# Stepping w_out's conversions at every slice behind the attention, with the PSUM banks split three and two

## The chip, the cores and the metric

The kernel runs on one core of one Trainium2 chip. The metric is the device time in microseconds of one execution; a lower time is better. The core has five engines with queues of their own, each of which runs its instructions strictly in the order in which the program gives them: TensorE (matmuls; its results go to PSUM, which has eight banks), VectorE, ScalarE, GpSimd, and SyncE, which starts most transfers. An engine whose next instruction waits for another engine stands still, whatever is queued behind.

## The reference, cut to what matters

Three layers in a row, on 2 batches of 768 tokens:

```python
# 1: retention ("attention"), 8 heads of 64
state = gamma * state + k[t] (outer) v[t];  y[t] = scale * q[t] @ state
# 2: gated feed-forward on x = y, d_model 512, d_ff 1024
h = relu(x @ w_in)
conv = sum(conv_w[k] * h[tokens shifted by k - 1] for k in range(3))
x2 = (h * sigmoid(conv)) @ w_out
# 3: top-1 mixture of 8 experts on x2, with a sticky choice:
#    a token takes argmax(x2 @ w_gate), or the expert of the token before it
#    where sigmoid(x2 @ w_local) >= 0.5
out = p[e] * (relu(x2 @ w1[e]) @ w2[e])
```

## The kernel before

Products run on values cut into a high and a low part (`hi`, `lo`), three matmuls for each product (`mm3`, lines 126 to 128). The order of all work is written out by hand: generators are stepped, and each step issues a few instructions.

**The pieces around the change.**
- `first = stream(0, range(8))` is the w_in product of batch 0: 8 blocks m of 128 hidden columns, each two halves `u` of 384 tokens, each of four slices (`ffn_in`, L347). A slice is one `mm3` of the 128x384 form; the fourth of a half is followed by ScalarE's relu (L357). A half takes one tile `h_ps` of the pool `psa`.
- Behind each slice `tick` steps `hidden(b, m)` (L327) for the blocks whose w_in product is done, at the slices TIMES = 0, 1, 3, 4, 10, 11, 13, 15 after it: ScalarE's first tap into `cc` (L331), two more taps on VectorE (L334), the sigmoid on ScalarE (L336), the product with h on VectorE (L338), the cut into `hg` high (ScalarE L307) and low (VectorE L311), and the router's logit on TensorE (`logit`, L325: eight matmuls). `cc` has two buffers. `logit` keeps a list `owed`: a block whose gate weights aren't in `ready` stays there until `logit` is called again.
- `convert` (L152) is one conversion of a 128x512 block of w_in or w_out from its 64-bit words: a load (three buffers `raw`), two VectorE instructions (L142, L143), one on ScalarE (L144), an addition on GpSimd (L146), the high part on ScalarE (L164), the low part on GpSimd (L166). Those of w_out (m = 0 to 7) go on: four transposes on TensorE into `wt_ps` (L175), ScalarE's copy to `wt` (L179), the product with the gate's weights into `wc_ps` (L183, eight matmuls), ScalarE's copy to `wc` (L185). The list `turning` lets one block at a time through this part. `wt_ps` and `wc_ps` have the same tag "g" in the pool `psg`. The numbers that a `convert` yields say after how many calls of `advance` it goes on.
- `advance` (L384) steps all conversions in `running` by one.

The attention's loop has 50 turns, each with one `advance`; from its turn 25 on, slices of `first` are put between (20 by its end). Then the attention's PSUM pools are closed and new ones opened: `psa` with 4 banks for `h_ps`, `psg` with 1, `psb` with 2 for w_out's product; one more bank holds the logits. The other 44 slices of `first` follow, with one `advance` behind every second one, then `while running: advance()` until no conversion is left.

After that come `stream(1, range(1))` (block 0 of batch 1, eight slices), `flush(0)` (the remaining `hidden` steps of batch 0), the w_out product of batch 0 (`ffn_out`, L454: first two token tiles over the blocks 0 to 5, then the rest) with `route(0)` between, `stream(1, range(1, 8))`, the same for batch 1 with `route(1)` and `tables()`, and the experts. `route` (L482) takes four tiles `sp` for the sticky choice from `psa` and `et` from `psg`; `tables` takes three from `psg`.

Of the kernel before, what the change touches and what calls it, by code (L numbers as in the profile page):

```python
# [9 lines left out]
F32 = mybir.dt.float32  # L10
# [6 lines left out]
PSUM = bass.MemoryType.PSUM  # L17
# [6 lines left out]
P = 128  # L24
# [60 lines left out]
def tile_kernel(ctx, tc, cat, cst, qT, kT, kN, vN, w_in, conv_w, w_out, wg, w1, w2, out):  # L85
# [4 lines left out]
    def pool(name, bufs, stack=ctx, **kw):  # L90
        return stack.enter_context(tc.tile_pool(name=name, bufs=bufs, reuse_waits="tile", **kw))

    def stack():
        return ctx.enter_context(ExitStack())
# [14 lines left out]
    psg = pool("psg", 1, ps_stack, space=PSUM)  # L109
    psa = pool("psa", 1, ps_stack, space=PSUM)  # L110
# [204 lines left out]
    def logit(*block):  # L315

        owed.extend(block)
        while owed and owed[0][1] in ready:
            b, m = owed.pop(0)
            if m == 0:  # L320
                LG[b] = psl.tile([P, NG, 32], F32, name="lg")
            x = CC.pop((b, m)).rearrange("p (t n) -> p t n", n=P)
            for i in range(4):
                o = slice(32 * i, 32 * i + 32)
                te.matmul(LG[b][o], wc[:, m, :], x[:, :, o], start=(m == 0), stop=(m == 7), skip_group_check=True)  # L325
# [58 lines left out]
    def advance():  # L384
        for r in list(running):
            r[1] -= 1
            if r[1] <= 0:
                r[1] = next(r[0], 0)
                if not r[1]:
                    running.remove(r)  # L390
# [42 lines left out]
        slices += 1  # L433
    ps_stack.close()
    q_stack = stack()
    psa = pool("psa", 4, q_stack, space=PSUM)
    psg = pool("psg", 1, q_stack, space=PSUM)
    psb = pool("psb", 2, q_stack, space=PSUM)
    n = 0
    for _ in first:  # L440
        n += 1
        if n % 2 == 0:
            advance()
    while running:
        advance()
    p1_stack.close()
# [35 lines left out]
    def route(b):  # L482

        logit(*[(b, m) for m in range(8) if (b, m) in CC and (b, m) not in owed])
        l = rt.tile([P, NG, 32], F32, name="l")
        ve.transpose(out=l.rearrange("p t e -> p (t e)"), in_=LG.pop(b).rearrange("p t e -> p (t e)"))
        wide = lambda a: a.unsqueeze(2).to_broadcast([P, NG, E])
        mx = rt.tile([P, NG], F32, name="mx")
        ve.tensor_reduce(out=mx, in_=l[:, :, 0:E], axis=AX.X, op=ALU.max)
        d = rt.tile([P, NG, E], F32, name="d")  # L490
        ve.tensor_tensor(out=d, in0=l[:, :, 0:E], in1=wide(mx), op=ALU.subtract)
        cd = rt.tile([P, NG, E], F32, name="cd")
        w8 = cs[:, C_W8:C_W8 + E].unsqueeze(1).to_broadcast([P, NG, E])
        ve.scalar_tensor_tensor(out=cd, in0=d, scalar=0.0, in1=w8, op0=ALU.is_ge, op1=ALU.mult)
        mc = rt.tile([P, NG], F32, name="mc")
        ve.tensor_reduce(out=mc, in_=cd, axis=AX.X, op=ALU.max)
        ve.tensor_tensor(out=cd, in0=cd, in1=wide(mc), op=ALU.is_equal)
        fr = rt.tile([P, NG, 1], F32, name="fr")
        s0 = cs[:, C_S0:C_S0 + NG].unsqueeze(2)
        ve.scalar_tensor_tensor(out=fr, in0=l[:, :, E:E + 1], scalar=FRESH, in1=s0, op0=ALU.is_le, op1=ALU.max)  # L500
        ab = rt.tile([P, 2, NG, E], F32R, name="ab")
        frb = fr.to_broadcast([P, NG, E])
        ve.tensor_tensor(out=ab[:, 0], in0=cd, in1=frb, op=ALU.mult)
        ve.tensor_scalar(out=ab[:, 1], in0=frb, scalar1=-1.0, scalar2=1.0, op0=ALU.mult, op1=ALU.add)
        ex = rt.tile([P, NG, E], F32, name="ex")
        se.activation(out=ex, in_=d, func=AF.Exp)
        yield
        sp = [[psa.tile([P, 512], F32, tag="a", name=f"sp{i}{u}") for u in range(2)] for i in range(2)]
        for i in (1, 0):
            for t in range(NG):  # L510
                te.matmul(sp[i][t // 3][0:E, (t % 3) * P:(t % 3 + 1) * P], ab[:, i, t, :], identr, start=True, stop=True)
        kp = rt.tile([E, S], F32, tag="kp", name="kp")
        for u in range(2):
            se.activation(out=kp[:, u * HF:(u + 1) * HF], in_=sp[1][u][0:E, 0:HF], func=AF.Copy)
        me = mr[0:E]
        mef = me.bitcast(F32)
        for u in range(2):
            us = slice(u * HF, (u + 1) * HF)
            ve.tensor_tensor_scan(out=me[:, us], data0=kp[:, us], data1=sp[0][u][0:E, 0:HF],
                                  initial=0.0 if u == 0 else mef[:, HF - 1:HF], op0=ALU.mult, op1=ALU.add)  # L520
        ve.tensor_tensor_scan(out=kp, data0=one.to_broadcast([E, S]), data1=mef, initial=carry, op0=ALU.mult, op1=ALU.add)
        ve.tensor_copy(out=carry, in_=kp[:, S - 1:S])
        yield
        ve.scalar_tensor_tensor(out=mr[RK:RK + E], in0=kp, scalar=-1.0, in1=mef, op0=ALU.add, op1=ALU.mult)
        sm = rt.tile([P, NG], F32, name="sm")
        ve.tensor_reduce(out=sm, in_=ex, axis=AX.X, op=ALU.add)
        ve.tensor_scalar(out=sm, in0=sm, scalar1=1e-9, scalar2=None, op0=ALU.add)
        ve.reciprocal(out=sm, in_=sm)
        yield
        et = psg.tile([P, NG, 10], F32, tag="g", name="et")  # L530
        for t in range(NG):
            ts = slice(t * P, (t + 1) * P)
            te.matmul(et[:, t, :], mr[:, ts], sel, start=True, stop=True)
        cc = slice(NG * b, NG * b + NG)
        pi = rt.tile([P, NG], I32, name="pi")
        pl = rt.tile([P, NG], I32, name="pl")
        ve.tensor_copy(out=pi, in_=et[:, :, E])
        ve.tensor_single_scalar(out=pl, in_=pi, scalar=P - 1, op=ALU.bitwise_and)
        ve.tensor_single_scalar(out=pi, in_=pi, scalar=-P, op=ALU.bitwise_and)
        ve.tensor_copy(out=base[:, cc], in_=pi)  # L540
        io = cs[:, C_IO:C_IO + P].unsqueeze(1).to_broadcast([P, NG, P])
        ve.tensor_tensor(out=one_p[:, cc, :], in0=io, in1=pl.unsqueeze(2).to_broadcast([P, NG, P]), op=ALU.is_equal)
        ve.tensor_tensor(out=ex, in0=ex, in1=et[:, :, 0:E], op=ALU.mult)
        ve.tensor_reduce(out=prob[:, cc], in_=ex, axis=AX.X, op=ALU.add)
        ve.tensor_tensor(out=prob[:, cc], in0=prob[:, cc], in1=sm, op=ALU.mult)
# [119 lines left out]
    for t in range(2):  # L665
        ffn_out(0, t, range(6))
    side = route(0)
    next(side)
    units = [(t, (6, 7)) for t in range(2)] + [(t, (m, m + 1)) for t in range(2, NG) for m in range(0, 8, 2)]
# [16 lines left out]
    for j in range(2):  # L686
        fetch(j, 0)
    side = route(1)
    next(side)
    cut(0, 0, 0)  # L690
# [19 lines left out]
    psa = pool("psc", 2, space=PSUM)  # L710
# [171 lines left out]
```

## Time and profile before

| | |
|---|---|
| median of 3 runs | 489.77 us (488.91 to 490.95) |
| profiled execution | 490.43 us, of which the span in the profile is 488.6 us |
| mean granted TensorE clock | 0.976 of full speed |
| busy in the span | TensorE 450.5 us, VectorE 351.3, ScalarE 318.3, GpSimd 128.6 |

Times in the profile count from the span's start. An engine's rows show a start, a duration and, in brackets, how long the engine had been idle before the instruction and what released it. Durations of successive instructions can overlap a little, so the cost of one in a row of them is the distance of the starts. The granted clock is given as a share of 2.4 GHz; its other level is 1.2 GHz. In the names PE is TensorE, DVE VectorE, ACT ScalarE, POOL GpSimd, PEld the loading of weights into TensorE.

### The profile page before, as it was taken

To read this page: it belongs to the slowest core of one execution; us is meant where nothing else is said; L and a number is where in the kernel's file an instruction comes from. 1 tells how busy PE (TensorE), PEld (TensorE's weight loads), DVE (VectorE), ACT (ScalarE), POOL (GpSimd) and SP (SyncE) were. 2 spreads that over 40 slices of the span, in tenths; PEclk is the share of its full clock that TensorE was granted. 3 is DMA by queue.
4 is the path that set the end of the run, shared out by engine and by line. 5 is a ranking of instruction groups with operands and counts; after the bars stand their busy time and mean duration, and the time that the engine had idled before them with its cause. 6 is when DMAs were issued, how large, how long until landed. Compare 5 with 4: busy or idle time off the path is not lost. (4 is left out here: it accounts for less than half of the span.)

```text
span 488.6 us, 7374 instructions
## 1 busy us (share of the span) xinstructions
PE 450.5 (92%) x2442; PEld 381.1 (78%) x2442; DVE 351.3 (72%) x550; ACT 318.3 (65%) x503; POOL 128.6 (26%) x113
## 2 busy tenths in 40 slices
PE   4988998896877999999898999999999999999995
PEld 3978988785775778987676888888888888888884
DVE  3798798787424261577853399999999999999952
ACT  3767775565534222666404399998888888888851
POOL 4456563442100000000002206632222222222001
PEclk9999999997978999999999899999999999999998
DMA  7998833200000111005402759971165106966401
GB/s 258 357 335 290 299 105 88 63 25 0 1 0 1 43 44 43 2 0 192 195 23 70 278 182 369 408 286 33 43 222 191 44 22 206 362 211 202 170 5 44
DMA packets 23351, 69.76 MB, mean 143 GB/s; under 512 B 3726, under 2 KB 4750, under 8 KB 23312
## 3 DMA queue, kind: packets, MB, share of 16 engines
q1 hardware_dynamic: 20592, 62.98, 36.2%
q0 software_dynamic: 2720, 6.30, 3.7%
q8 instruction: 20, 0.33, 0.3%
q14 instruction: 19, 0.16, 0.1%
HBM read 97.84 MB, written 7.60 MB: 216 GB/s over the span
## 5 line engine op out<-in xcount | busy, mean ns | idle before, releaser
L334 DVE SCALAR_TENSOR_TENSOR cc<-h,cw,cc 128x768 f32<-128x768 f32 x32 | 36.5, 1139 | 37.5 <-ACT cc L331 37.5
L779 POOL DMA_INDIRECT out_dram<-yo,it x17 | 22.7, 1336 | 148.9 <-ACT yo L778 135.4
L640 DVE TENSOR_TENSOR wc<-r,wc 128x1024 fp32r<-128x1024 f32 x44 | 51.8, 1220 | 1.4 <-ACT wc L639 0.8
L126 PE MATMUL h_ps<-xT,wih 128*128 128x384 f32 x128 | 47.8, 373 | 0.0
L649 POOL DMA_INDIRECT xg<-xs,it x17 | 33.9, 1996 | 45.9 <-issue 40.1
L639 ACT ACTIVATE wc<-r 128x1024 fp32r<-128x1024 f32 x44 | 44.5, 1071 | 0.0
L127 PE MATMUL h_ps<-xT,wih 128*128 128x384 f32 x128 | 44.3, 346 | 0.0
L128 PE MATMUL h_ps<-xT,wil 128*128 128x384 f32 x128 | 44.3, 346 | 0.0
L126 PE MATMUL x_ps<-woh,hg 128*128 128x512 f32 x96 | 39.3, 409 | 0.0
L127 PE MATMUL x_ps<-wol,hg 128*128 128x512 f32 x96 | 38.2, 398 | 0.0
L128 PE MATMUL x_ps<-woh,hg 128*128 128x512 f32 x96 | 38.2, 398 | 0.0
L263 PE MATMUL s_ps<-qz,kq 128*128 128x256 f32 x96 | 31.0, 408 | 6.2 <-DMA kq<-in_kT_dram 3.5
L648 POOL MEMSET xg<- 128x512 f32 x17 | 9.2, 542 | 94.4 <-DVE cc L338 94.4
L640 DVE TENSOR_TENSOR ws0h<-r,ws0h 128x1024 fp32r<-128x1024 f32 x24 | 28.3, 1221 | 7.5 <-ACT ws0h L639 6.9
L281 PE MATMUL y<-at,vz 128*128 128x128 f32 x192 | 31.3, 287 | 0.9 <-DVE xT L286 0.6
L640 DVE TENSOR_TENSOR ws0l<-r,ws0l 128x1024 fp32r<-128x1024 f32 x24 | 28.3, 1219 | 3.4 <-ACT ws0l L639 3.4
L146 POOL TENSOR_TENSOR na<-na,raw 128x512 int32<-128x512 int32 (+1 forms) x17 | 23.3, 1369 | 28.1 <-DVE na L143 11.1
L469 ACT ACTIVATE xn<-x_ps 128x512 f32<-128x512 f32 x11 | 6.6, 597 | 36.7 <-PE x_ps L128 29.0
L767 ACT ACTIVATE hr<-g 128x512 f32<-128x512 f32 x34 | 18.5, 598 | 17.5 <-PE g L128 14.5
L640 DVE TENSOR_TENSOR ws1l<-r,ws1l 128x1024 fp32r<-128x1024 f32 x22 | 26.0, 1222 | 5.4 <-ACT ws1l L639 4.9
L265 DVE TENSOR_TENSOR at<-s_ps,ca 128x256 f32<-128x256 f32 x48 | 20.1, 420 | 12.2 <-PE s_ps L263 12.2
L281 PEld LDWEIGHTS y<-at,vz 128*128 128x128 f32 x192 | 26.3, 197 | 3.2 <-DVE xT L286 2.3
(208 smaller groups left out, 1283.5 us busy)
## 6 DMA issues: line engine op xcount, KB each, us to landing
r<-in_w_dram SPq DMA_DIRECT2D x136, 512.0 KB
raw<-in_w_in_dram SPq DMA_DIRECT2D x8, 512.0 KB
raw<-in_w_out_dram SPq DMA_DIRECT2D x8, 512.0 KB
xs<-xn SPq DMA_DIRECT2D x11, 256.0 KB
kq<-in_qT_dram SPq DMA_DIRECT2D x7, 384.0 KB
kq<-in_kT_dram SPq DMA_DIRECT2D x7, 384.0 KB
kv<-in_vN_dram SPq DMA_DIRECT2D x7, 384.0 KB
kv<-in_kN_dram SPq DMA_DIRECT2D x7, 384.0 KB
```

Of the source, the lines that this page charges most:

```text
L126: te.matmul(ps, lhi, rhi, start=first, stop=False)
L127: te.matmul(ps, lhi, rlo, start=False, stop=False)
L128: te.matmul(ps, llo, rhi, start=False, stop=last)
L146: po.tensor_tensor(out=a, in0=a, in1=lo, op=ALU.add)
L263: te.matmul(ps, self.kq[:, 0, tok], self.qz[:, :, tok], start=True, stop=True)
L265: ve.tensor_tensor(out=self.at[c], in0=ps, in1=self.dm, op=ALU.mult)
L281: te.matmul(y, vz[:, c, j, :], at[:, j, :], start=(j == 0), stop=(c == 0 and j == 1))
L334: ve.scalar_tensor_tensor(out=cc, in0=h[:, i:i + S], scalar=cw[:, m, i:i + 1], in1=cc, op0=ALU.mult, op1=ALU.add)
L639: se.activation(out=w[:, 0, h, :], in_=r, func=AF.Copy)
L640: ve.tensor_tensor(out=w[:, 1, h, :], in0=r, in1=w[:, 0, h, :].bitcast(F32), op=ALU.subtract)
L649: return po.indirect_dma_start(out=xg, out_offset=None, in_=xs[0:n], in_offset=bass.IndirectOffsetOnAxis(ap=it[:, j:j + 1], axis=0), bound ...
L779: po.indirect_dma_start(out=out, out_offset=bass.IndirectOffsetOnAxis(ap=it[:, j:j + 1], axis=0), in_=yo, in_offset=None, bounds_check=NT ...
```

## The change

Behind the attention, `advance` is called after every slice and no more after every second one. The pools that open there have 3 banks in `psa` and 2 in `psg` (before: 4 and 1), so `wt_ps` and `wc_ps` take turns in two banks. As `route` then finds only three banks in `psa`, the first of its four tiles `sp` goes to `psg`.

```diff
     q_stack = stack()
-    psa = pool("psa", 4, q_stack, space=PSUM)
-    psg = pool("psg", 1, q_stack, space=PSUM)
+    psa = pool("psa", 3, q_stack, space=PSUM)
+    psg = pool("psg", 2, q_stack, space=PSUM)
     psb = pool("psb", 2, q_stack, space=PSUM)
-    n = 0
     for _ in first:
-        n += 1
-        if n % 2 == 0:
-            advance()
+        advance()
     while running:
         advance()
...
-        sp = [[psa.tile([P, 512], F32, tag="a", name=f"sp{i}{u}") for u in range(2)] for i in range(2)]
+        sp = [[(psa if i + u else psg).tile([P, 512], F32, tag="a" if i + u else "g", name=f"sp{i}{u}") for u in range(2)] for i in range(2)]
```

## Rows read from the trace of the kernel before

**Rows 1.** Windows by stage: stretch, length, busy of each engine, clock, DMA share, GB/s

```profile
90.70:144.10 53.40, 41.78 (x263) 36.57 (x263) 32.98 (x35) 28.84 (x51) 15.74 (x9) 0.90 0.04 11
144.10:153.90 9.80, 6.82 (x42) 5.89 (x42) 2.43 (x3) 1.62 (x4) 0.00 (x0) 0.84 0.00 0
153.90:230.00 76.10, 75.41 (x412) 63.64 (x409) 39.27 (x58) 34.74 (x51) 0.53 (x1) 0.98 0.12 41
```

**Rows 2.** Waits of TensorE from 90.6 to 154 us: total, times, longest

```profile
PE wt_ps L175 <- ACT wc L185: 8.4, 6, 3.2
...
PE wc_ps L183 <- ACT wt L179: 3.1, 3, 1.6
```

**Rows 3.** Timeline of TensorE: start, duration, instruction, idle before and releaser

```profile
92.32 0.33 PE L126 MATMUL h_ps<-xT,wih 128*128 128x384 f32 x1
...
93.36 0.95 PE L183 MATMUL wc_ps<-wgs,wt 128*128 128x9 f32 x8
94.17 0.42 PE L126 MATMUL h_ps<-xT,wih 128*128 128x384 f32 x1
...
97.82 0.63 PE L175 MATMUL wt_ps<-cs,na 128*128 128x128 f32 x4 [1.90 <-ACT wc L185]
98.20 0.42 PE L126 MATMUL h_ps<-xT,wih 128*128 128x384 f32 x1
...
102.55 0.53 PE L325 MATMUL lg<-cc,wc 128*32 128x192 f32 x8
...
118.64 1.09 PE L175 MATMUL wt_ps<-cs,na 128*128 128x128 f32 x4 [3.17 <-ACT wc L185]
...
123.45 0.53 PE L325 MATMUL lg<-cc,wc 128*32 128x192 f32 x8
...
137.78 0.63 PE L175 MATMUL wt_ps<-cs,na 128*128 128x128 f32 x4 [0.74 <-ACT wc L185]
...
153.41 0.53 PE L325 MATMUL lg<-cc,wc 128*32 128x192 f32 x8 [2.98 <-DVE cc L338]
...
153.88 0.66 PE L126 MATMUL x_ps<-woh,hg 128*128 128x512 f32 x1
...
157.63 0.40 PE L126 MATMUL x_ps<-woh,hg 128*128 128x512 f32 x1
```

**Rows 4.** Timeline of ScalarE, behind the attention and before w_out's product

```profile
96.39 0.84 ACT L336 ACTIVATE cc<-cc 128x768 f32<-128x768 f32 x1 [1.13 <-DVE cc L334]
97.14 0.47 ACT L357 ACTIVATE h<-h_ps 128x384 f32<-128x384 f32 x1
...
97.64 0.94 ACT L331 ACTIVATE cc<-h,cw 128x768 f32<-128x768 f32 x1
98.49 0.66 ACT L144 ACTIVATE raw<-raw 128x512 int32<-128x512 uint32 x1
...
102.36 0.58 ACT L179 ACTIVATE wt<-wt_ps 128x512 f32<-128x512 f32 x1
102.83 0.62 ACT L164 ACTIVATE woh<-na 128x512 fp32r<-128x512 f32 x1
...
150.50 0.94 ACT L331 ACTIVATE cc<-h,cw 128x768 f32<-128x768 f32 x1 [6.00 <-PE lg L325]
```

**Rows 5.** Timeline of VectorE in the same stretch

```profile
94.29 2.06 DVE L334 SCALAR_TENSOR_TENSOR cc<-h,cw,cc 128x768 f32<-128x768 f32 x1
...
98.61 1.02 DVE L334 SCALAR_TENSOR_TENSOR cc<-h,cw,cc 128x768 f32<-128x768 f32 x1 [1.39 <-ACT cc L331]
99.55 0.42 DVE L142 TENSOR_SCALAR na<-raw 128x512 int32<-128x512 int32 x1
100.01 0.69 DVE L143 SCALAR_TENSOR_TENSOR na<-raw,na 128x512 int32<-128x512 int32 x1
100.61 0.95 DVE L338 TENSOR_TENSOR cc<-cc,h 128x768 f32<-128x768 f32 x1
```

**Rows 6.** Timeline of GpSimd at the same time

```profile
93.52 2.02 POOL L146 TENSOR_TENSOR na<-na,raw 128x512 int32<-128x512 int32 x1
```

## The prediction

> **What bounds the kernel now.** I read the windows by stage first. From 153.9 us on TensorE is busy 75.41 of 76.1 us [rows 1]: what starts that part earlier ends the kernel earlier. The two windows ahead of it are different. From 90.7 to 144.1 us TensorE is busy 41.78 of 53.4 us at a mean granted clock of 0.90, and from 144.1 to 153.9 only 6.82 of 9.8 at 0.84. VectorE (32.98) and ScalarE (28.84) aren't full there either: three engines wait for each other in order. So I read next what TensorE waits for there: 8.4 us, in 6 places, at the transposes of the next w_out block for ScalarE's copy of the gate's product of the block before (L185), and 3.1 us at the gate's product for ScalarE's copy of the transposed block (L179) [rows 2]. The first is the single bank "g". ScalarE itself is late: at 97.82 TensorE has waited 1.90 us, because that copy stands behind a sigmoid that began only at 96.39, after a 2.06 us VectorE instruction [rows 3 to 5].
>
> The third reading is the order at the end of the stretch. Counting the yields of the conversions, 44 slices of the w_in product follow the attention. With a step at every second slice, conversions 6 and 7 are left over: they run alone after the last slice, a chain of transposes, copy, product, copy, twice. Block 5's logit misses its turn, since its gate weights aren't ready, and is next tried with block 6's, eight slices into batch 1. Block 7's first `hidden` step needs the buffer that block 5 holds: at 150.50 ScalarE has waited 6.00 us for that logit [rows 4]. Through ScalarE's queue this holds VectorE back, and the second logit is reached at 153.41 after 2.98 us of idle TensorE, at a clock that has fallen [rows 3].
>
> **The change part by part.** No instruction is added or removed. What moves is the place of conversions 1 to 7 among the slices (their TensorE, ScalarE, VectorE and GpSimd instructions together), and which bank each tile gets. By the count of yields a conversion takes five steps from its transposes to the next ones, so five slices in place of ten; the seventh ends in block 6, every conversion is done when the loop ends, and logit 5 goes out with block 7's last slice. Nothing is left to run alone. The last raw load isn't moved in effect: it waits for its buffer in SP's queue in both orders, and nothing stands behind it there until the stores of the second product.
>
> *TensorE's work* from 92.32 us, where the 44 slices begin, to w_out's first product: eight slices take 98.20 to 102.55, less a small gap 0.53 each; a gate's product 0.81 (93.36 to 94.17); four transposes 0.38 (97.82 to 98.20); a logit's eight matmuls 0.5 [rows 3]. With 44 slices and batch 1's first 8: 52 x 0.53 = 27.6; 7 products 5.7; 6 sets of transposes 2.3; 7 logits 3.5; together 39.1 us, so 131.4 with no wait at all.
>
> *The waits.* With two banks, a block's transposes need only that the copy of the block before has been read, three slices earlier. The 8.4 us as such go. But the product now comes two slices, 1.1 us, behind ScalarE's copy in program order in place of four, so TensorE is held to ScalarE's queue there. I place the first two by the rows. ScalarE is as before until its sigmoid at 96.39 (ends for the next at 97.14); relu with the gate copy 0.50 (to 97.64), conversion 0.6, the copy of block 2 0.47 (102.36 to 102.83), hi part 0.5, `cc` 0.85 (97.64 to 98.49) [rows 4]. The copy of block 2 is done at 98.7 and `cc` at 100.05. TensorE wants it at 97.2 (six slices, one product, one set of transposes and a logit from 92.32): a wait of 1.5. Then VectorE: first tap from 100.15. Here three of the next four VectorE instructions run beside GpSimd, which has five conversion instructions in this place. What that costs is in the rows: 2.06 us for the tap at 94.29 beside a GpSimd instruction at 93.52, 1.02 us for the one at 98.61 alone [rows 5, 6]. So the tap 2.0, the gating product 1.9 (0.95 alone), conversion 6's two instructions 1.1 (0.42 + 0.69), the second tap 2.0: 107.1; ScalarE's sigmoid 0.75 and the copy of block 3 0.47: 108.3. TensorE has been ready from 102.5. The wait is 5.8 us, or 3 us if nothing collides; I take the upper end, because the order puts a GpSimd instruction beside each of the three. It also needs all of them: `cc` of the next block is queued on ScalarE behind this copy, so VectorE stands too. For the later ones the same placing gives nothing, 0.2, 0.8, nothing: GpSimd has only three instructions left. Waits together: 8.3 us.
>
> *The clock.* After a wait of 3.17 us the transposes at 118.64 ran 1.09 us in place of 0.63, and the stretch to 123.45 took 4.81 us where transposes and 12 matmuls of the other clock take 2.6 [rows 3]: 2.2 us at the lower level, 1.2 GHz. A wait of 5.8 us will do the same, so I add 2.2; the lower bound is 0. TensorE: Matmul & The Clock Gate in the Trainium skill (HAM oscillation) says that idle gaps between bursts put the clock back to half, and what was just read agrees; by the rule the 2.2 stands, without it the sum would be 2.2 shorter. On the other side w_out's first product starts cold today: nine matmuls from 153.88 to 157.63, 3.75 us [rows 3]. At twice the clock it is about half; I take 1.7 us, and they come back, since TensorE runs on without a long gap from 117 us.
>
> *Three banks for the w_in product, `sp00` in "g".* Batch 1's product lies in the third window, in which TensorE lacks 0.7 us in all [rows 1]. A bank is wanted again two halves (eight slices, 4.2 us) after its own half ends, and a relu stands behind little more than one `cc` (0.94) and a sigmoid (0.84) [rows 4]. Nothing is lost; without this cover a wait of half a us in 14 halves would be 7 us. `sp00` takes a bank whose last reader is long done: nothing, at most half a us in each of two routings.
>
> **Sum.** 92.32 + 39.1 + 8.3 + 2.2 = 141.9, in place of 153.88: 12.0 us earlier, and 1.7 from the warm start: 13.7 us. The span goes from 488.6 to 474.9; the profiled execution had 490.43, so 1.83 us lie around it: 476.7. The median of the runs stands 0.66 under that execution: **476.0 us**.
>
> A check from the other side: if the 44 slices keep today's pace and end at 137 us as they do now (the transposes at 137.78 follow 0.74 of waiting [rows 3]), with two more conversions among them (2 x 1.2), then 8 slices and a logit come out at 144.2: 9.7 us and 1.7, a time of 478.4. The tail alone is most of the gain.
>
> **The rivals.**
> *No waits left* (the banks do all): 131.4 in place of 153.88 and the warm start, 24.2 us, 465.6. For it speaks that the 8.4 us stand at the bank; against it that ScalarE and VectorE are late there on their own. Trace Analysis in the Trainium skill (Optimizing Tensor Performance, Matmuls) wants independent groups in different banks, so that evacuation overlaps the next group; by that alone this is the case to come. The trace does not agree as a whole: 3.1 us of waits are no bank's.
> *The long wait comes two or three times* (conversions 4 and 5 as well): 6 to 7 us more for each: 482 with two, 489 with three, which is no gain.
> *Slower: the copy's wait at every conversion.* Five products of 5.8 us each and the low clock in between: 131.4 + 1.5 + 29 + 4 = 165.9, 12 later, less the warm start: 500 us. It decides from some 4 us a wait, where five of them with 1.5 and 2.2 use up the 24 us. For it: the steps come twice as dense, and VectorE and GpSimd collide. Against it: GpSimd's nine instructions then lie within three blocks, and the later blocks have VectorE to themselves.
> *No change*: what TensorE saves, it waits for VectorE. VectorE is busy 32.98 of 53.4 us; it would need the pace of today and a new chain as long as the tail. I see none.
>
> **Numbers.** The forecast, with its own range of 470 to 481: 0.70. No or hardly any wait (under 470): 0.10. Two or three long waits, still faster: 0.11. About as before: 0.04. Slower: 0.05. The range is 468 to 482. Half a per cent, 2.4 us, is about what can be told from no change here: faster 0.91, same 0.04, slower 0.05.
>
> **What would show it.** Right: w_out's first product of batch 0 starts near 142 us; no gap before it of over 2 us but one of 3 to 6 near 103 at a gate's product (L183), released by the copy L179; logit 5 ahead of batch 1's first slice; no 6 us of ScalarE before a `cc`; a clock of 1.00 from 144 on. Wrong: several gaps of over 3 us at L183, relus waited for by the w_in product in batch 1, or TensorE below 75 us in the 76 after w_out's start.

## The result and the profile after

The changed kernel takes 476.96 us (median of 4 runs, 475.95 to 477.34); the kernel before took 489.76 beside it. The ratio is 0.9734, with a 95% interval of 0.9708 to 0.9759. The forecast was 476.0 us. The profiled execution took 477.34 us with a span of 475.5 (before: 490.43 and 488.6).

Windows of the changed kernel: the stretch behind the attention cut at the places where it changes, then 76 us from w_out's first product on (columns as in [rows 1]).

```profile
90.70:98.00 7.30, 6.88 (x49) 5.97 (x47) 7.27 (x8) 4.41 (x9) 3.70 (x2) 1.00 0.20 55
98.00:102.00 4.00, 3.32 (x19) 3.28 (x20) 2.19 (x3) 3.13 (x7) 3.54 (x3) 0.80 0.10 37
102.00:107.00 5.00, 2.48 (x10) 2.16 (x8) 4.97 (x5) 2.55 (x4) 2.79 (x2) 0.82 0.00 0
107.00:112.00 5.00, 4.83 (x24) 3.79 (x25) 0.72 (x1) 2.41 (x6) 1.27 (x1) 0.52 0.00 0
112.00:115.00 3.00, 3.00 (x15) 3.00 (x13) 2.83 (x4) 0.67 (x2) 1.48 (x1) 0.66 0.00 0
115.00:143.00 28.00, 27.25 (x194) 23.90 (x192) 17.85 (x21) 17.59 (x31) 1.91 (x2) 1.00 0.01 1
...
142.00:218.00 76.00, 75.34 (x422) 63.27 (x420) 39.76 (x58) 35.25 (x52) 0.53 (x1) 1.00 0.12 43
```

The later part runs as before: 75.34 of 76 us. All that changed lies ahead of it, and there one place stands out: from 102 to 107 VectorE is full (4.97 of 5 us) and TensorE half empty, and behind it the clock is at its lower level.

TensorE's waits from 90.6 to 150 us are one line now; the 8.4 us at the transposes of [rows 2] are gone:

```profile
PE wc_ps L183 <- ACT wt L179: 4.6, 3, 2.7
```

The timeline of TensorE shows where:

```profile
98.68 1.06 PE L183 MATMUL wc_ps<-wgs,wt 128*128 128x9 f32 x8 [1.10 <-ACT wt L179]
...
100.22 0.87 PE L175 MATMUL wt_ps<-cs,na 128*128 128x128 f32 x4
...
104.14 0.34 PE L128 MATMUL h_ps<-xT,wil 128*128 128x384 f32 x1
107.17 1.86 PE L183 MATMUL wc_ps<-wgs,wt 128*128 128x9 f32 x8 [2.70 <-ACT wt L179]
...
113.76 0.48 PE L126 MATMUL h_ps<-xT,wih 128*128 128x384 f32 x1
...
124.42 1.06 PE L183 MATMUL wc_ps<-wgs,wt 128*128 128x9 f32 x8 [0.76 <-ACT wt L179]
...
137.70 0.53 PE L325 MATMUL lg<-cc,wc 128*32 128x192 f32 x8
142.53 0.53 PE L325 MATMUL lg<-cc,wc 128*32 128x192 f32 x8
142.99 0.50 PE L126 MATMUL x_ps<-woh,hg 128*128 128x512 f32 x1
143.33 0.40 PE L127 MATMUL x_ps<-wol,hg 128*128 128x512 f32 x1
...
145.16 0.39 PE L126 MATMUL x_ps<-woh,hg 128*128 128x512 f32 x1
```

w_out's first product starts at 142.99 in place of 153.88 [rows 3], and its second matmul takes 0.40 us: the clock is up. Its first nine matmuls take 2.17 us (142.99 to 145.16) in place of 3.75. Block 5's logit (137.70) stands ahead of batch 1's eight slices.

VectorE and then GpSimd around the long wait:

```profile
100.01 1.80 DVE L334 SCALAR_TENSOR_TENSOR cc<-h,cw,cc 128x768 f32<-128x768 f32 x1 [1.81 <-ACT cc L331]
101.74 2.02 DVE L338 TENSOR_TENSOR cc<-cc,h 128x768 f32<-128x768 f32 x1
103.69 0.41 DVE L142 TENSOR_SCALAR na<-raw 128x512 int32<-128x512 int32 x1
104.13 0.69 DVE L143 SCALAR_TENSOR_TENSOR na<-raw,na 128x512 int32<-128x512 int32 x1
104.74 1.01 DVE L334 SCALAR_TENSOR_TENSOR cc<-h,cw,cc 128x768 f32<-128x768 f32 x1
105.67 2.05 DVE L311 TENSOR_TENSOR hg<-cc,hg 128x768 fp32r<-128x768 f32 x1
```

```profile
98.46 1.29 POOL L146 TENSOR_TENSOR na<-na,raw 128x512 int32<-128x512 int32 x1 [3.01 <-DVE na L143]
99.71 3.24 POOL L166 TENSOR_TENSOR wol<-na,woh 128x512 fp32r<-128x512 f32 x2
105.06 1.84 POOL L146 TENSOR_TENSOR na<-na,raw 128x512 int32<-128x512 int32 x1 [2.11 <-DVE na L143]
```

Beside the two subtractions (99.71 to 102.95) the tap takes 1.80 us and the gating product 2.02. The second tap at 104.74 began before GpSimd's next addition and took 1.01; the addition then took 1.84 in place of the 1.29 that it takes at 98.46, where VectorE stood. The cut at 105.67 began while the addition ran and took 2.05. The rows read as if the two took turns: the tap ends at 105.75, the addition 1.15 later (106.90), the cut 0.82 after that (107.72), so each ends about its own time behind the end of the one before. No run tests this reading by itself.

### The profile page after: what moved, and what is told of

Read it like the earlier page. It is cut to its first block, busy times and chain, and to the rows that moved or that the text cites. A ratio compares the mean times of both kernels' runs of the same rounds, so it can differ in the third digit from the quotient of the medians.

```text
span 475.5 us, 7373 instructions
## 1 busy us (share of the span) xinstructions
PE 447.7 (94%) x2442; PEld 378.6 (80%) x2442; DVE 351.1 (74%) x550; ACT 317.3 (67%) x503; POOL 127.5 (27%) x113
## 5 line engine op out<-in xcount | busy, mean ns | idle before, releaser
L334 DVE SCALAR_TENSOR_TENSOR cc<-h,cw,cc 128x768 f32<-128x768 f32 x32 | 35.1, 1098 | 21.2 <-ACT cc L331 21.2
L126 PE MATMUL x_ps<-woh,hg 128*128 128x512 f32 x96 | 38.7, 403 | 0.0
L128 PE MATMUL x_ps<-woh,hg 128*128 128x512 f32 x96 | 37.6, 392 | 0.0
L281 PE MATMUL y<-at,vz 128*128 128x128 f32 x192 | 31.1, 284 | 1.4 <-DVE xT L286 0.6
L357 ACT ACTIVATE h<-h_ps 128x384 f32<-128x384 f32 x32 | 15.6, 486 | 20.7 <-PE h_ps L128 18.5
L281 PEld LDWEIGHTS y<-at,vz 128*128 128x128 f32 x192 | 26.0, 195 | 3.9 <-DVE xT L286 2.4
```

Source lines behind the costliest of these rows:

```text
L126: te.matmul(ps, lhi, rhi, start=first, stop=False)
L128: te.matmul(ps, llo, rhi, start=False, stop=last)
L281: te.matmul(y, vz[:, c, j, :], at[:, j, :], start=(j == 0), stop=(c == 0 and j == 1))
L334: ve.scalar_tensor_tensor(out=cc, in0=h[:, i:i + S], scalar=cw[:, m, i:i + 1], in1=cc, op0=ALU.mult, op1=ALU.add)
```

## The experiments

**One part at a time.** `step_only` is the kernel before with the step at every slice and the old banks:

```diff
-    n = 0
     for _ in first:
-        n += 1
-        if n % 2 == 0:
-            advance()
+        advance()
```

> The kernel before with the step at every slice alone; the banks stay four and one. My theory (the conversions' end after the last slice is most of the gain; the waits inside belong to ScalarE's late queue, which the bank only names): 477.5 to 479.5 us, 0.5 to 2.5 above the changed kernel, w_out's first product at 143 to 146, a short wait for the gate product's copy L185 at the second transposes, and the long wait at the third gate product still there. Rival (the second bank is needed, the denser steps run into the one bank at each conversion): 483 us or more, waits at L175 of over 6 us in all.

Measured 480.83 us, ratio 0.9833 (0.9798 to 0.9868). Its waits of TensorE:

```profile
PE wt_ps L175 <- ACT wc L185: 5.1, 2, 3.0
PE wc_ps L183 <- ACT wt L179: 3.2, 2, 2.5
```

Neither came: it is 1.3 us above my range and 2.2 below the rival's. The transposes of block 2 are held where I had them held, but for 2.98 us and not shortly. Slices behind them are held too, and ScalarE's copy of block 2 (100.34, in the changed kernel 98.04) stands behind the relu of such a slice, so the delay goes round:

```profile
97.69 0.63 PE L175 MATMUL wt_ps<-cs,na 128*128 128x128 f32 x4 [2.98 <-ACT wc L185]
```

```profile
99.95 0.49 ACT L357 ACTIVATE h<-h_ps 128x384 f32<-128x384 f32 x1 [1.83 <-PE h_ps L128]
100.34 0.59 ACT L179 ACTIVATE wt<-wt_ps 128x512 f32<-128x512 f32 x1
```

Its w_out starts at 147.01, 4.0 later than with both parts.

`banks_only` has the changed banks with a step at every second slice:

> The changed banks with a step at every second slice as before. My theory: the chain after the last slice and block 5's late logit stay, so w_out's product starts at 149 to 151; the 7.3 us of waits at the transposes inside the slices go, and part of them comes back at the gate products (L183 for the copy L179): 485 to 488 us. Rival (independent banks let the copies overlap, so all of the 8.4 us are gained): 481 to 482 us.

Measured 480.96 us, ratio 0.9819 (0.9797 to 0.9841): the rival's figure, within the noise. Its windows show why my size was wrong:

```profile
90.70:137.00 46.30, 38.98 (x270) 34.96 (x271) 33.46 (x36) 28.86 (x53) 15.77 (x9) 1.00 0.04 12
137.00:146.40 9.40, 6.42 (x39) 5.50 (x37) 2.38 (x3) 1.40 (x3) 0.00 (x0) 0.82 0.00 0
```

Waits do come back among the slices, at logits (1.25 us the longest) and at gate products (1.46 the longest), but none is long, and the clock holds 1.00 to 137 us, where it was 0.90 [rows 1]. The conversions left over are shorter too: 131.95 to 136.51, against 137.0 to 144.1. The late logit is untouched: the second logit still waits 2.98 us, at 145.96, and w_out still starts into the lower clock:

```profile
146.42 0.50 PE L126 MATMUL x_ps<-woh,hg 128*128 128x512 f32 x1
...
147.27 0.63 PE L126 MATMUL x_ps<-woh,hg 128*128 128x512 f32 x1
```

Each part alone is worth 9 us; together they give 12.8.

`logit_early` is the kernel before and one line:

```diff
     while running:
         advance()
+    logit()
```

> The kernel before with one line more: the list of owed logits is tried again right after the last conversion, ahead of batch 1's first slices. My theory (block 7's first hidden step waits for block 5's buffer, and that costs TensorE the wait ahead of 153.41 and the cold start of w_out): the first tap stands near 145 in place of 150.50, w_out starts near 150, 484 to 486 us. Rival (the logit is late but TensorE is held by the chain of taps anyway): 488.5 us or more.

Measured 484.8 us, ratio 0.9881 (0.9851 to 0.9911), as expected. Block 7's first tap goes out at 144.93 in place of 150.50, and w_out starts at 151.38 (I had put it near 150) at the full clock. So the late logit alone cost some 5 us of the kernel before, through ScalarE's queue and the buffer of `cc`.

**What makes the long wait.** `late_low` takes GpSimd's subtraction of the blocks 4 to 7 out of the crowded place (and gives the narrowed words four buffers):

```diff
+        late = m is not None and m >= 4
+        if not late:
             po.tensor_tensor(out=lo, in0=w, in1=hi.bitcast(F32), op=ALU.subtract)
...
         se.activation(out=wc[:, m, 0:E + 1], in_=pg, func=AF.Copy)
+        if late:
+            po.tensor_tensor(out=lo, in0=w, in1=hi.bitcast(F32), op=ALU.subtract)
```

> The changed kernel with GpSimd's subtraction (L166) of the w_out blocks 4 to 7 put behind their own gate product, and four in place of three buffers for the narrowed words. My theory (the long wait at the third gate product is VectorE slowed by GpSimd): the tap and the gating product near 100 to 104 take 1.0 and 0.95 us in place of 1.80 and 2.02, the wait shrinks by about 2 us, and the time falls by 1 to 3 us to 474 to 476. Rival (the wait is the order of ScalarE's queue, whatever VectorE's speed): within 0.7 us of the changed kernel, 476.3 to 477.6.

Measured 474.61 us, ratio 0.9693 (0.9677 to 0.9709). VectorE at the same place:

```profile
99.92 1.02 DVE L338 SCALAR_TENSOR_TENSOR cc<-h,cw,cc 128x768 f32<-128x768 f32 x1 [1.82 <-ACT cc L335]
100.86 0.95 DVE L342 TENSOR_TENSOR cc<-cc,h 128x768 f32<-128x768 f32 x1
```

1.02 and 0.95 us in place of 1.80 and 2.02, and the third gate product starts at 105.22 in place of 107.17. The tap starts where it did (99.92, against 100.01), so these two instructions account for 1.85 of the 1.95 us: this part of the wait is VectorE beside GpSimd. The profile is of the fastest execution (472.13 us); by the medians the kernel gains 2.4 us.

The four late subtractions have not gone away. GpSimd does them in one go later, and there too they double VectorE's instructions:

```profile
109.44 7.89 POOL L189 TENSOR_TENSOR wol<-na,woh 128x512 fp32r<-128x512 f32 x4
```

```profile
110.22 2.04 DVE L342 TENSOR_TENSOR cc<-cc,h 128x768 f32<-128x768 f32 x1
112.19 2.03 DVE L338 SCALAR_TENSOR_TENSOR cc<-h,cw,cc 128x768 f32<-128x768 f32 x1
114.14 2.05 DVE L315 TENSOR_TENSOR hg<-cc,hg 128x768 fp32r<-128x768 f32 x1
```

In this place it costs TensorE no wait: the next copy of a block is ready at 115.6, and TensorE, part of the way at the lower clock, comes to the product only at 116.04.

`late34` puts the step at three of four slices on top of `late_low`:

> The kernel with GpSimd's late low parts (474.61) and the step at three of four slices together. My theory (two different causes of the same wait, so both count, the second less): 472.5 to 474.2 us, waits at the gate product under 2 us and no low clock before w_out. Rival (one wait, removed once): 474 to 475.

Measured 477.67 us, ratio 0.9738 (0.9717 to 0.976): no gain over the changed kernel, and outside my range and the rival's. The four late subtractions again go in one go, and here the collision falls ahead of a copy that TensorE waits for:

```profile
111.50 7.15 POOL L189 TENSOR_TENSOR wol<-na,woh 128x512 fp32r<-128x512 f32 x4
```

```profile
113.45 2.12 DVE L338 SCALAR_TENSOR_TENSOR cc<-h,cw,cc 128x768 f32<-128x768 f32 x1 [1.09 <-ACT cc L335]
115.50 2.04 DVE L342 TENSOR_TENSOR cc<-cc,h 128x768 f32<-128x768 f32 x1
117.46 2.01 DVE L338 SCALAR_TENSOR_TENSOR cc<-h,cw,cc 128x768 f32<-128x768 f32 x1
```

Three in a row are doubled, as in `late_low`, but the sigmoid and the copy behind them on ScalarE come late (the copy at 120.26), and the fifth gate product waits 4.36 us. The collision had moved, not gone.

**The clock.** `filler` puts idle matmuls ahead of the third gate product of the changed kernel:

```diff
+        if m == 3:
+            fl = psb.tile([P, DM], F32, tag="x2", name="fill")
+            for k in range(32):
+                te.matmul(fl[:, 0:HF], identr, xT[0, 0][:, 0, 0:HF], start=True, stop=True)
         pg = psg.tile([P, E + 1], F32, tag="g", name="wc_ps")
```

> The changed kernel with 32 idle matmuls of 384 columns (some 5.4 us, their result is read by nobody) put ahead of the third gate product, where TensorE waits 2.70 us by the waits and stands from 101.5 to 107.2 in all. My theory (the low clock behind that wait costs some 2 us, as the step of the prediction said): the clock stays at 1.00, the gate product at 107 takes about 1.0 us in place of 1.86, w_out starts near 141, 474.5 to 475.5 us. Rival (TensorE at the low clock only used time that ScalarE and VectorE needed anyway): within 0.7 us of the changed kernel's 476.96.

Measured 476.11 us, ratio 0.9716 (0.9688 to 0.9744); between my range and the rival's, and by time it can't be told from the changed kernel. The profile tells more: the fill was too long (TensorE stood from 104.3 and not from 101.5; until then it did slices at the lower clock). It ends at 108.55, and the product would have gone near 107.2; the clock is 1.00 throughout, and w_out starts at 141.60, 1.4 earlier in spite of it. `late_fill` does the same on `late_low`, with 22 matmuls:

> The kernel with GpSimd's late low parts (474.61) and 22 idle matmuls ahead of the third gate product, for the 3.7 us in which TensorE stands there. By my theory the low clock from 105 to 109 goes: 472.5 to 473.8. Rival: within 0.5 us of 474.61.

Measured 475.28 us, ratio 0.9686 (0.9662 to 0.9711), no difference from `late_low`: the fill took 3.9 us (103.99 to 107.87), and the wait that it was to cover is 0.84. So what the low clock costs in time is not shown by these two; both fills were too long.

**How dense the steps.** `three_of_four` is the changed kernel with a step at three of four slices (`if n % 4: advance()`):

> The changed kernel with a step at three of four slices (33 steps, just what the conversions need to end with the loop). My theory (a gate product waits because its copy stands only two slices ahead of it and ScalarE is late): the waits at L183 fall from 4.6 to 2 to 3 us, 474.5 to 476.5 us. Rival (ScalarE and VectorE set the pace whatever the density): within 0.5 us of 476.96.

Measured 474.97 us, ratio 0.9672 (0.9644 to 0.97): the time as expected, the reason not. The waits at the gate product rose from 4.6 to 6.3 us, the longest 2.24, but the clock stayed at 1.00. So I took the clock for the cause and ran it again beside the changed kernel:

> The step at three of four slices with the changed banks, once more with five rounds beside the changed kernel. Theory formed after its first run (its waits are no fewer, 6.3 us in all, but none is long and the clock stays at 1.00, so what it saves is the low clock): 0.966 to 0.969, 2 to 3 us below the changed kernel on the same chip, and again a clock of 1.00 from 90.7 to 145 us. Rival (the first run was chance): no more than 1 us below it.

> The changed kernel once more, to stand on the same chip as the next one. 0.972 to 0.975.

Measured 474.35 us, 0.9688 (0.966 to 0.9716), for `three_again` and 477.29 us, 0.9729 (0.9713 to 0.9745), for `after_again`: the gain is there again, though one of the six executions (477.94) took as long as the changed kernel. The clock of 1.00 that I had expected did not come. In this profile it fell (0.96 from 90.7 to 135 us), but the waits were 4.7 us. Neither number alone ranks the kernels; their sum does better (below).

`three_one_bank` has the three-of-four steps with the old banks:

> The kernel before with the step at three of four slices and its banks as they were, four and one. If the second bank matters at the gentler density too: waits at the transposes for the gate product's copy (L185) of 4 to 6 us in all, ratio 0.979 to 0.984 against 0.9672 with the changed banks. Rival (the bank matters only where a block follows the other at the densest): under 2 us of such waits, ratio 0.970 or below.

Measured 480.49 us, ratio 0.9795 (0.9772 to 0.9818), with 6.2 us of waits at the transposes: the second bank matters at this density as well.

`product_later` lets the gate product come three steps behind the copy:

```diff
         se.activation(out=wt, in_=ps, func=AF.Copy)
-        yield 2
+        yield 2 if m < 2 else 3
```

> The changed kernel in which a gate product comes three steps behind ScalarE's copy in place of two (blocks 2 to 7), so that TensorE has one more slice to do before it can wait. My theory (TensorE is held at the product by ScalarE's queue): the wait ends at the same moment with 0.5 us more work done, at two or three places; ratio to the kernel before 0.970 to 0.9725, where the changed kernel had 0.9734. Rival (the pace is VectorE's, and the extra slice is only paid earlier): 0.973 to 0.975.

Measured 474.36 us, ratio 0.9674 (0.966 to 0.9688), more than expected: 2.9 us below the changed kernel on the same chip, and level with `three_again` (474.35) and `late_low`. Its third gate product waits 1.46 us and the longest wait is that one. Its profile (the fastest execution, 472.17 us) has hardly less waiting than the changed kernel's, 4.1 us against 4.5, but less low clock. That isn't the whole reason: two other executions of it had a mean clock of 0.988 and took 474.18 and 474.37 us, where the changed kernel at 0.988 took 476.03 to 477.51 beside it. Where those two gained isn't shown, as they were not profiled.

**One account for all.** The windows from 90.7 to 135 us of four of them (the column behind the five engines is the mean clock), in the order `product_later`, `three_again`, `after_again`, `step_only`:

```profile
90.70:135.00 44.30, 40.22 (x274) 35.61 (x273) 31.92 (x35) 28.18 (x53) 14.33 (x9) 0.96 0.04 13
```

```profile
90.70:135.00 44.30, 39.63 (x267) 35.12 (x269) 33.63 (x34) 28.39 (x52) 14.79 (x9) 0.96 0.05 13
```

```profile
90.70:135.00 44.30, 39.76 (x249) 35.23 (x248) 29.12 (x30) 25.81 (x48) 14.69 (x9) 0.88 0.05 13
```

```profile
90.70:135.00 44.30, 35.96 (x224) 31.36 (x223) 27.05 (x28) 22.95 (x44) 14.18 (x9) 0.88 0.04 13
```

The clock's loss is 44.3 times what its mean lacks to 1.00. The stretch is counted from the attention's last set of products (L281) to w_out's first.

| kernel | stretch, us | waits of TensorE | clock's loss | rest |
|---|---|---|---|---|
| product_later | 49.5 | 4.1 | 1.8 | 43.6 |
| late_low | 49.7 | 2.7 | 3.5 | 43.5 |
| three_again | 50.2 | 4.7 | 1.8 | 43.7 |
| three_of_four | 50.3 | 6.3 | 0 | 44.0 |
| filler (and 5.6 of fill) | 51.4 | 2.1 | 0 | 43.7 |
| after_again | 53.0 | 4.5 | 5.3 | 43.2 |
| three_one_bank | 55.4 | 8.2 | 3.5 | 43.7 |
| step_only | 56.7 | 8.3 | 5.3 | 43.1 |

The rest is the same work in all, 43.1 to 44.0 us. Reckoned in the same way, the other six traces of this document come to 42.3 to 43.8 (lowest, the kernel before and `logit_early`, whose clock was low for longest, also while TensorE waited, so that some time counts twice). It is bookkeeping of one execution each, and those of `late_low` and `product_later` were 2.5 and 2.2 us faster than their medians. What a version gains in the stretch is waits plus clock, and one can take the place of the other: a slower TensorE reaches the next wait later and waits less. Of `three_of_four` and `three_again`, the same program, the second had the low clock ahead of the fifth gate product and waited 0.65 us there, the first 2.24.

## Why the prediction was right

**The place and the moved work.** Right: no conversion is left at the loop's end, logit 5 goes out at 137.70, no wait of 2.98 us ahead of w_out. w_out's start was forecast at 141.9 and came at 142.99.

**The waits.** The bank's waits are gone. The wait at the second product was put at 1.5 and is 1.10. The long one is where it was said and, for the part that `late_low` takes away, for the reason given. It was put at 5.8 us and measured 2.70, which is under the 3 to 6 us that the prediction named as its sign. Its end was forecast at 108.3 and is 107.17: two of the three collisions came as placed, the third fell on the cut behind the second tap and so off the chain. Some 1.8 us more of the difference is that TensorE itself came later (next paragraph). The later waits were put at 0, 0.2, 0.8, 0; the profile has one, 0.76.

**The clock.** Under-sized. It falls twice, not once. The first time (the transposes at 100.22 take 0.87 us, full speed is back at 103.76) adds nothing to the end of the wait, which ScalarE's copy sets: TensorE only reaches it at 104.3 in place of 102.5. The second, from 107.17 to 113.76, takes 6.6 us for a product, a set of transposes, a logit and nine matmuls of slices, 3.3 by the prediction's prices: 3.3 us, not 2.2. The Trainium skill's rule that gaps between bursts bring the lower level back (TensorE: Matmul & The Clock Gate, HAM oscillation) held in these rows, behind waits of 1.10 and 2.70 us. In `three_of_four` waits of up to 2.24 us left the clock at 1.00. That the whole loss adds to the sum did not hold.

**The sum.** From the end of the long wait to w_out 35.8 us against 33.6 forecast: 1.1 for the clock, the rest in changes between kinds of matmul, which were priced as if each kind ran alone (the slice behind a product took 0.61 us, 115.76 to 116.37, not 0.53). The earlier end of the wait gave 1.1 back, so w_out's start is off by 1.1. That the sum fits so well is in part luck. From the start of the 44 slices (92.27) to w_out the waits are 4.6 us where 8.3 were forecast, the two stretches of low clock cost TensorE 1.6 and 3.3 us where 2.2 were, and the work is then 41.3 us where 39.1 were: one term too high and two too low.

**Behind it.** The warm start of w_out is there: its first nine matmuls take 1.6 us less (1.7 forecast). The span behind w_out's start can't show it so closely: it is 334.7 us before and 332.5 now, but the kernels here with a warm start spread from 330.8 to 333.0, and `banks_only` without one has 332.8. Three banks cost the w_in product nothing, and `sp` waits 0.3 us as before.

**What was wrong beside the forecast:** the check that ends in the sentence that the tail alone is most of the gain. It put the tail at 11.4 us with the warm start; `step_only`, which drops the tail and keeps the one bank, gains 8.9, and `banks_only`, which keeps the tail, gains 8.8: either part alone gives two thirds of the 12.8. They overlap by some 5 us. Some of it can be read off: the second bank shortens the leftover conversions too (by 2.5 us), which the denser steps do away with, and without the denser steps it holds the clock at 1.00 to 137 us, while with them the low clock is back (5.3 us in the changed kernel). How much of the 5 us each makes isn't shown. The rival with no waits left did not come, even in the best version; the rule that stood beside it (the Trainium skill's Perfetto Trace Analysis, Matmuls) is borne out for the 8.4 us at the bank and not for the 4.6 us at the product, which belong to a late ScalarE.

## What to carry to other kernels

Where TensorE must pass through another engine in the middle of its stream, ask which instructions stand ahead of that engine's answer in its own queue; a second bank frees the next group, and one slice more between request and use was worth another 2.9 us (474.36 against 477.29 beside it). Work put out to GpSimd has its place in the order too: in the changed kernel two subtractions at 99.71 double two of VectorE's instructions, and the next one, at 107.71, finds VectorE idle and costs nothing. Moving such work paid where no copy that TensorE waited for stood behind the new collision (`late_low`), and not where one did (`late34`). Price a version by waits and clock together, over the whole stretch; neither alone ranks them.

## What the runs showed of the hardware that was not expected

- Lower clock and waiting can stand in for each other: `three_of_four` and `three_again`, the same program, lost 6.3 + 0 and 4.7 + 1.8 us in one stretch and that stretch came out within 0.1 us. The same program at nearly the same gaps (2.04 us ahead of the fourth gate product in both) kept 1.00 in one execution and had a mean of 0.96 in the other.
- VectorE's two-input instructions on 768 elements took 1.8 to 2.1 us where a GpSimd instruction was already under way and 0.95 to 1.02 otherwise in the rows shown; a GpSimd addition that began during a VectorE tap took 1.84 in place of 1.29. The kernel before has the same: VectorE's cut at 103.48 took 0.95 us, and the GpSimd subtraction that began at 103.53 took 2.03. So the later of the two pays, and the prediction's third collision missed the second tap because that tap began first. The Trainium skill's GPSIMD Engine Reference (Specifications) says that GpSimd's interfaces to the on-chip memory are shared with VectorE, with contention for VectorE instructions with two inputs there; the traces agree.
